# Loading q, k and v as float32 on the SP queue with casts on chip, and moving the x transposes a step earlier, in an attention-then-mixing kernel

## The chip, the cores and the metric

The kernel runs on one core of one Trainium2 chip. The metric is the device time of that core in microseconds (us), lower is better. Times are medians of several runs of the same kernel. The experiments ran in four sets on four chips, each set beside the kernel before on the same chip. A run more than 1.5% above the fastest of its kernel counts as slow and is left out. A profile covers one execution; its span, from the first to the last instruction, is about 1.7 us shorter than the time of the same execution (358.8 against 360.54 us in the changed kernel).

Names used below: PE is TensorE, PEld its weight load, DVE is VectorE, ACT is ScalarE, POOL is GpSimd, SP is SyncE (here it only issues transfers). Of the tiles, `ip` is a constant (an identity and the columns that average over 4 tokens), `pstr` is q or k transposed, `pd` the exponentials of the pooled attention and `xd` its output, `psS` the local attention scores, `pm` their exponentials, which GpSimd masks with two "selects" each, `psloc` the local attention output, `x` the sum of both attentions, `xT` its transpose, `psth` the theta product, `cs` its cosine and sine, `z` is x times `cs`, `psu` the mixing over tokens, `uT` the sum of mixing and xT, `psr` the last product.

## The reference

Eight batches, 8 heads, 576 tokens, head size 64. Two attentions are added, then a mixing layer follows:

```python
# attention 1: q, k, v averaged over groups of 4 tokens, full softmax attention, repeated 4 times
q_d = q.reshape(B, H, Sd, 4, D).mean(axis=3)          # the same for k, v
out_up = np.repeat(sm_attn(q_d, k_d, v_d), 4, axis=2)
# attention 2: local, a token sees the tokens at a distance under 4
mask = np.abs(pos[:, None] - pos[None, :]) < 4
out_local = softmax(where(mask, q @ k.T / 8, -1e9)) @ v
x = (out_up + out_local).transpose(0, 2, 1, 3).reshape(B, S, H * D)
# the mixing layer
theta = x @ w_theta
y = w_tok_r @ (x * cos(theta)) + w_tok_i @ (x * sin(theta))
u = x + y
return u + maximum(u @ w_ch, 0)
```

All inputs and the output are float32. The kernel computes in bfloat16 with float32 accumulation.

## The kernel before

Attention of batch b+1, `modulate` of batch b (theta and z) and `mix` of batch b-1 are three generators, interleaved in the fixed order of `PERIOD`: m, a and x stand for one step of `modulate`, `attention` and `mix`. The parts that the change and the argument touch:

```python
    def load(b):
        q_tm = work.tile([TR, NTR, H, D], BF16, tag="q_tm", name=f"q_tm{b}")
        k_tm = work.tile([TR, NTR, H, D], BF16, tag="k_tm", name=f"k_tm{b}")
        v_w = work.tile([P, NCH, H, 66], BF16, tag="v_w", name=f"v_w{b}")
        for dst, src in ((q_tm, q), (k_tm, k)):
            for c in range(NTR):
                nc.gpsimd.dma_start(
                    out=dst[:, c, :, :],
                    in_=src[b, :, TR * c:TR * c + TR, :].rearrange("h p d -> p h d"),
                )
        for c in range(NCH):
            nc.gpsimd.dma_start(
                out=v_w[0:KW[c], c, :, 0:D],
                in_=v[b, :, KS[c]:KS[c] + KW[c], :].rearrange("h p d -> p h d"),
            )
        nc.vector.memset(v_w[:, :, :, 64:65], 1.0)
        return q_tm, k_tm, v_w

    inputs = {0: load(0)}

    ident = const.tile([P, P], BF16, name="ident")
    nc.gpsimd.memset(ident, 0.0)
    nc.gpsimd.affine_select(out=ident, in_=ident, compare_op=ALU.not_equal, fill=1.0,
                            base=0, pattern=[[-1, P]], channel_multiplier=1)

    ip = const.tile([TR, TW], BF16, name="ip")
    nc.vector.tensor_copy(out=ip[:, 0:TR], in_=ident[0:TR, 0:TR])
    nc.gpsimd.memset(ip[:, TR:TW], 0.25)
    nc.gpsimd.affine_select(out=ip[:, TR:TW], in_=ip[:, TR:TW], compare_op=ALU.is_ge, fill=0.0,
                            base=0, pattern=[[-4, TP]], channel_multiplier=1)
    nc.gpsimd.affine_select(out=ip[:, TR:TW], in_=ip[:, TR:TW], compare_op=ALU.is_ge, fill=0.0,
                            base=3, pattern=[[4, TP]], channel_multiplier=-1)
    # ... pooling matrices PM and repeat matrices RT: 6 and 2 tiles, 24 + 4 selects on GpSimd ...
    wth = wpool.tile([P, 4, DM], BF16, name="wth")
    nc.gpsimd.dma_start(out=wth, in_=moe_w_theta.rearrange("(c p) e -> p c e", p=P))
    wtmp = ctx.enter_context(tc.tile_pool(name="wtmp", bufs=1))
    w_tm = []
    for ri, w_dram in enumerate((moe_w_tok_r, moe_w_tok_i)):
        t = wtmp.tile([P, 5, S], BF16, name=f"wtm{ri}")
        nc.gpsimd.dma_start(out=t[:, 0:4, :], in_=w_dram[0:512, :].rearrange("(c p) e -> p c e", p=P))
        nc.gpsimd.dma_start(out=t[0:64, 4, :], in_=w_dram[512:576, :])
        w_tm.append(t)
    wch = wpool.tile([P, 4, DM], BF16, name="wch")
    nc.gpsimd.dma_start(out=wch, in_=moe_w_ch.rearrange("(c p) e -> p c e", p=P))
```

The transfers that GpSimd issues here turn float32 into bfloat16 on their way: a piece of q lands as 96 KB, where the changed kernel's float32 piece has 192 KB. In `attention`, the local scores are masked like this, and only then multiplied with v:

```python
    def attention(b):
        q_tm, k_tm, v_w = inputs.pop(b)
        if b + 1 < B:
            inputs[b + 1] = load(b + 1)
        # ... transposes pstr, pooled attention ...
        for c in range(NCH):
            # ... psS matmuls, pm = exp(psS) on ACT ...
            nc.gpsimd.affine_select(out=pm[0:kw, :, 0:qn], in_=pm[0:kw, :, 0:qn],
                                    compare_op=ALU.is_ge, fill=0.0,
                                    base=off, pattern=[[0, 8], [-1, qn]], channel_multiplier=1)
            nc.gpsimd.affine_select(out=pm[0:kw, :, 0:qn], in_=pm[0:kw, :, 0:qn],
                                    compare_op=ALU.is_ge, fill=0.0,
                                    base=6 - off, pattern=[[0, 8], [1, qn]], channel_multiplier=-1)
            pms.append(pm)
            yield
        # ... psnd; then for each of 5 blocks psup, psloc, rl, tmp, x ...
```

The transposes of x, theta and z, and the order of a period:

```python
    def modulate(b):
        xT = moep.tile([P, 4, S], BF16, tag="xT", bufs=3, name=f"xT{b}")
        z = moep.tile([P, NCH, 2, DM], BF16, tag="z", name=f"z{b}")
        state[b] = (xT, z)
        xt = xs.pop(b)
        for c in range(NCH):
            cnt = QC[c]
            ps = w1(f"xTps{c}_{b}", BF16)[:, 0:512].rearrange("p (e t) -> p e t", e=4)
            for dc in range(4):
                nc.tensor.transpose(
                    out=ps[:, dc, 0:cnt],
                    in_=xt[c][0:cnt, P * dc:P * dc + P],
                    identity=ident[0:cnt, 0:cnt],
                )
            nc.vector.tensor_copy(out=xT[:, :, QS[c]:QS[c] + cnt], in_=ps[:, :, 0:cnt])
            yield
            th = w1(f"psth{c}_{b}")
            for dc in range(4):
                nc.tensor.matmul(
                    out=th[0:cnt, :],
                    lhsT=xT[:, dc, QS[c]:QS[c] + cnt],
                    rhs=wth[:, dc, :],
                    start=(dc == 0), stop=(dc == 3),
                )
            cs = moep.tile([P, 2, DM], BF16, tag="cs", bufs=3, name=f"cs{c}_{b}")
            nc.scalar.activation(out=cs[0:cnt, 0, :], in_=th[0:cnt], func=AF.Sin, bias=pihc[0:cnt], scale=1.0)
            nc.scalar.activation(out=cs[0:cnt, 1, :], in_=th[0:cnt], func=AF.Sin, bias=0.0, scale=1.0)
            nc.vector.tensor_tensor(
                out=z[0:cnt, c, :, :], in0=cs[0:cnt],
                in1=xt[c][0:cnt].unsqueeze(1).to_broadcast([cnt, 2, DM]),
                op=ALU.mult,
            )
            yield

    PERIOD = (
        "m a a m x m a a m x m a a m x m a a m x m a m "
        "a x a a a x a a x a a x a x a x a a x a a x a a x a x a"
    ).split()
    # ...
    a0 = attention(0)
    wt = build_WT()
    for _ in range(10):
        next(a0, 0)
        next(wt, 0)
    drain(wt)
    drain(a0)
    for b in range(B + 1):
        run(attention(b + 1) if b + 1 < B else None,
            modulate(b) if b < B else None,
            mix(b - 1) if b >= 1 else None)
```

The softmax here doesn't subtract the row's maximum and nothing guards it: scores larger than these inputs give would overflow.

## Time and profile before

The median is 365.32 us (four runs, 365.04 to 365.76). I cut the span at the first `psth` of each batch. That gives a start-up, seven periods, and a tail; in each period the attention of one batch, the theta of the one before and the mixing of the one before that are done together.

This is the view of busy time by stretch of the kernel before, for the start-up, the first period and one steady period. The columns are from:to, length, then the busy time of PE, PEld, DVE, ACT and POOL with the number of instructions, the mean granted PE clock (1.00 is full), the DMA engines' busy time as a share of the stretch (it can read over 1, as 1.19 and 1.35 below), and GB/s.

```profile
0.00:61.80 61.80, 27.81 (x247) 20.37 (x248) 15.64 (x43) 14.12 (x19) 53.23 (x98) 0.88 1.19 99
61.80:92.50 30.70, 23.16 (x239) 16.18 (x236) 16.69 (x41) 20.61 (x31) 30.59 (x37) 0.72 1.35 86
...
206.98:244.29 37.31, 33.77 (x346) 22.67 (x349) 21.70 (x53) 24.00 (x36) 23.56 (x28) 1.00 0.85 80
```

In the steady period PE is busy 33.77 of 37.31 us, and no other engine is near that. So PE sets the pace there, and what counts is where PE waits. In the start-up POOL is the busy one. GpSimd's own transfer issues are counted as busy here: of its 28 instructions in the steady period ten are selects, the rest issues.

The view of waits of the kernel before (who waited for whom, us in all, times, longest) shows the two waits that the change aims at: theta waits for the copy of the transposed x, and the very first transposes wait for a constant that GpSimd builds late.

```profile
PE pstr L177 <- POOL ip L102: 16.6, 1, 16.6
PE psth L352 <- DVE xT L348: 14.2, 15, 1.9
```

The timeline of its start (start, us, engine, line, operation, tile) shows why that constant is late: GpSimd issues 17 loads first.

```profile
1.37 4.74 POOL L77 DMA_DIRECT2D q_tm<-in_q_dram  x6 [0.84 <-POOLq L457]
...
10.63 4.48 POOL L82 DMA_DIRECT2D v_w<-in_v_dram  x5
...
16.64 1.36 PE L177 MATMUL pstr<-ip,q_tm 96*128 96x120 bf16 x12 [16.64 <-POOL ip L102]
...
24.77 0.79 POOL L136 DMA_DIRECT2D wth<-in_moe_w_theta_dram  x1
...
49.93 2.19 POOL L260 TENSOR_SCALAR_AFFINE_SELECT pm<-pm 128x1024 bf16<-128x1024 bf16 x2
```

Last, the chain of waits in the first period of the kernel before. ACT works almost without a break from 62.8 us on; the last of it, from the table load at 74.29, is below. Then come the selects, with a single load issue between them.

```profile
74.29 1.28 ACT L224
...
75.59 1.67 ACT pd L224 x2
...
77.79 1.03 ACT pm L254
...
78.89 2.13 POOL pm L260 x2
...
88.05 0.73 POOL k_tm L77
88.78 0.85 POOL pm L263
```

### The profile page before, as it was taken

What the parts mean: (1) busy time and instruction counts of PE and PEld (TensorE: products, weight loads), DVE (VectorE), ACT (ScalarE), POOL (GpSimd) and SP (SyncE); (2) the same over time, 40 slices, a digit from 0 to 9 for tenths busy, and PEclk for the clock granted to TensorE, in tenths of its full rate; (3) what the DMA queues carried; (4) which work ended last, traced back from release to release, by engine and by line L of the source; (5) the groups of instructions that cost most, each with busy time, mean ns of one, the idle gap of its engine ahead of it and who ended that gap; (6) DMA issues with size and microseconds to landing.
All of it is one profiled execution on the core that took longest, in us unless ns stands there. A gap on an engine that the chain in (4) does not pass through costs nothing.

```text
span 363.3 us, 6945 instructions
## 1 busy us (share of the span) xinstructions
PE 293.9 (81%) x2820; PEld 199.3 (55%) x2834; DVE 180.7 (50%) x428; ACT 191.3 (53%) x280; POOL 202.5 (56%) x267
## 2 busy tenths in 40 slices
PE   0162966948989978997999799979997899789995
PEld 0152643636665656565656465647564666456672
DVE  0020327617451875277536853594449444934433
ACT  1070331990569366845685567646774677323303
POOL 8996599999873957395639655870073006400000
PEclk9999955975699999999999999999999999989999
DMA  9909993991997199919991699057002000300303
GB/s 77 121 6 189 167 100 26 125 127 11 114 83 49 60 133 82 60 60 118 89 65 60 98 112 65 31 109 63 2 24 93 16 0 3 117 16 2 115 16 131
DMA packets 123392, 26.65 MB, mean 73 GB/s; under 512 B 116576, under 2 KB 118752, under 8 KB 123360
## 3 DMA queue, kind: packets, MB, share of 16 engines
q0 software_dynamic: 118112, 16.77, 66.7%
q1 hardware_dynamic: 5248, 9.44, 7.2%
q8 instruction: 22, 0.36, 0.4%
q14 instruction: 10, 0.08, 0.1%
HBM read 33.51 MB, written 9.44 MB: 118 GB/s over the span
## 4 chain that ended last, share of the span: by engine, by line
PE 45%; DVE 17%; ACT 15%; POOL 14%; issue 4%; DMA 4%; DVEq 0%; POOLq 0%
PE psu L377 16%; PE psth L352 10%; PE psr L395 5%; DVE tmp L319 4%; DVE osb L407 4%; DMA wch<-in_moe_w_ch_dram 4%; ACT pd L224 3%; DVE x L326 3%; ACT cs L359 3%; PE psS L247 3%; POOL pm L260 3%; POOL k_tm L77 3%; ACT L224 2%; PE pstr L177 2%; PE psvd L199 2%
## 5 line engine op out<-in xcount | busy, mean ns | idle before, releaser
L377 PE MATMUL psu<-WT,z 122*128 122x288 bf16 (+1 forms) x640 | 94.2, 292 | 0.0
L260 POOL TENSOR_SCALAR_AFFINE_SELECT pm<-pm 128x1024 bf16<-128x1024 bf16 (+1 forms) x40 | 40.7, 1038 | 71.4 <-ACT pm L254 71.3
L377 PEld LDWEIGHTS <-z 122*128 122x128 bf16 (+1 forms) x640 | 60.0, 99 | 23.8 <-issue 0.5
L352 PE MATMUL psth<-wth,xT 128*122 128x512 bf16 (+1 forms) x160 | 44.6, 402 | 14.2 <-DVE xT L348 14.2
L405 ACT ACTIVATE rel<-psr 128x512 f32<-128x512 f32 (+1 forms) x40 | 23.8, 596 | 57.4 <-PE psr L395 57.4
L386 DVE TENSOR_TENSOR uT<-psu,xT 128x288 bf16<-128x288 f32 x64 | 27.3, 454 | 53.2 <-PE psu L377 53.2
L184 ACT CAST qT<-pstr 128x576 bf16<-128x576 f32 x32 | 19.8, 640 | 55.6 <-PE pstr L177 55.6
L77 POOL DMA_DIRECT2D q_tm<-in_q_dram x48 | 37.0, 789 | 15.4 <-PE pstr L177 10.0
L361 DVE TENSOR_TENSOR z<-cs,x 122x1024 bf16<-122x1024 bf16 (+1 forms) x40 | 27.4, 686 | 34.3 <-ACT cs L360 34.3
L77 POOL DMA_DIRECT2D k_tm<-in_k_dram x48 | 36.8, 779 | 13.0 <-PE pstr L177 10.1
L395 PE MATMUL psr<-wch,uT 128*128 128x512 bf16 (+1 forms) x146 | 40.5, 380 | 2.3 <-DVE x L326 1.6
L254 ACT ACTIVATE pm<-psS 128x1024 bf16<-128x1024 f32 (+1 forms) x40 | 35.3, 976 | 12.5 <-PE psS L247 12.0
L263 POOL TENSOR_SCALAR_AFFINE_SELECT pm<-pm 128x1024 bf16<-128x1024 bf16 (+1 forms) x40 | 40.7, 1038 | 0.4
L82 POOL DMA_DIRECT2D v_w<-in_v_dram x40 | 35.4, 913 | 9.7 <-PE psloc L310 7.3
L359 ACT ACTIVATE cs<-psth,pihc 122x512 bf16<-122x512 f32 (+1 forms) x40 | 27.6, 691 | 23.7 <-PE psth L352 23.3
L352 PEld LDWEIGHTS <-xT 128*122 128x122 bf16 (+1 forms) x160 | 18.4, 135 | 26.4 <-DVE xT L348 18.3
L177 PE MATMUL pstr<-ip,q_tm 96*128 96x120 bf16 x192 | 16.4, 236 | 19.7 <-POOL ip L102 16.6
L407 DVE TENSOR_TENSOR osb<-rel,psx 128x512 f32<-128x512 f32 (+1 forms) x40 | 27.3, 682 | 7.9 <-ACT rel L405 7.1
L319 DVE TENSOR_TENSOR tmp<-psloc,rl 122x512 bf16<-122x512 f32 (+1 forms) x40 | 26.5, 687 | 0.3
L310 PEld LDWEIGHTS <-pm 128*128 128x128 bf16 (+1 forms) x320 | 17.0, 112 | 17.3 <-POOL pm L263 8.0
L348 DVE COPY xT<-xTps 128x488 bf16<-128x488 bf16 (+1 forms) x40 | 15.6, 391 | 21.1 <-PE xTps L343 21.1
L326 DVE TENSOR_TENSOR x<-tmp,psup 122x512 bf16<-122x512 bf16 (+1 forms) x40 | 25.9, 673 | 0.0
(62 smaller groups left out, 407.8 us busy)
## 6 DMA issues: line engine op xcount, KB each, us to landing
out_dram<-osb SPq DMA_DIRECT2D x32, 256.0 KB, 2.0
q_tm<-in_q_dram POOLq DMA_DIRECT2D x48, 96.0 KB, 3.7
k_tm<-in_k_dram POOLq DMA_DIRECT2D x48, 96.0 KB, 3.7
v_w<-in_v_dram POOLq DMA_DIRECT2D x32, 128.0 KB, 4.7
out_dram<-osb SPq DMA_DIRECT2D x8, 128.0 KB, 3.2
v_w<-in_v_dram POOLq DMA_DIRECT2D x8, 91.0 KB, 5.3
wtm<-in_moe_w_tok_r_dram POOLq DMA_DIRECT2D x1, 576.0 KB, 8.4
wtm<-in_moe_w_tok_i_dram POOLq DMA_DIRECT2D x1, 576.0 KB, 10.3
```

The lines of the kernel that those rows point to most:

```text
L77: nc.gpsimd.dma_start(out=dst[:, c, :, :], in_=src[b, :, TR * c:TR * c + TR, :].rearrange("h p d -> p h d"),)
L82: nc.gpsimd.dma_start(out=v_w[0:KW[c], c, :, 0:D], in_=v[b, :, KS[c]:KS[c] + KW[c], :].rearrange("h p d -> p h d"),)
L254: nc.scalar.activation(out=pm[0:kw, :, 0:qn], in_=ps[0:kw].rearrange("p e (j w) -> p (e j) w", w=P)[:, :, 0:qn], func=AF.Exp, scale=SCL,)
L260: nc.gpsimd.affine_select(out=pm[0:kw, :, 0:qn], in_=pm[0:kw, :, 0:qn], compare_op=ALU.is_ge, fill=0.0, base=off, pattern=[[0, 8], [-1, qn ...
L263: nc.gpsimd.affine_select(out=pm[0:kw, :, 0:qn], in_=pm[0:kw, :, 0:qn], compare_op=ALU.is_ge, fill=0.0, base=6 - off, pattern=[[0, 8], [1, ...
L319: nc.vector.tensor_tensor(out=tmp[0:cnt].rearrange("p (j e d) -> p e j d", e=2, j=4), in0=pv[0:cnt, :, :, 0:D], in1=rl[0:cnt].unsqueeze(3) ...
L326: nc.vector.tensor_tensor(out=x[0:cnt], in0=tmp[0:cnt], in1=up[0:cnt], op=ALU.add)
L352: nc.tensor.matmul(out=th[0:cnt, :], lhsT=xT[:, dc, QS[c]:QS[c] + cnt], rhs=wth[:, dc, :], start=(dc == 0), stop=(dc == 3),)
L359: nc.scalar.activation(out=cs[0:cnt, 0, :], in_=th[0:cnt], func=AF.Sin, bias=pihc[0:cnt], scale=1.0)
L377: nc.tensor.matmul(out=pss[hf][:, 0:288], lhsT=z[0:QC[c], c, ri, P * dc:P * dc + P], rhs=WT[0:QC[c], ri, c, 288 * hf:288 * hf + 288], star ...
L395: nc.tensor.matmul(out=psr[0:cnt, :], lhsT=uT[:, dc, OS[c]:OS[c] + cnt], rhs=wch[:, dc, :], start=(dc == 0), stop=(dc == 3),)
L407: nc.vector.tensor_tensor(out=osb[0:cnt], in0=rel[0:cnt], in1=psx[0:cnt, 0:DM], op=ALU.add)
```

## The change

It has four parts. The loads of q, k and v go to the SP queue as float32 into staging tiles. They are cast on chip: for batch 0 by VectorE, GpSimd and ScalarE, for the other batches by GpSimd. That frees GpSimd of 17 load issues a batch. The constants are built as three tiles, two pooling matrices (`PU`) and one repeat matrix (`ru`), which replace the eight old ones with the help of shifted views. The views need blocks of 120 tokens, which replace those of 122. And the transposes of x run one step ahead of theta, with a new `PERIOD`, so that theta need not wait for the copy of its own transposes.

```diff
-QS = [0, 122, 244, 366, 488]
+QS = [0, 120, 240, 360, 480]
 (QC, KS, KW, QN likewise)
 ...
-    def load(b):
-        (17 nc.gpsimd.dma_start a batch, into bfloat16 tiles)
+    def load_qk(b):
+        ts = []
+        for nm, src in (("q", q), ("k", k)):
+            t = work.tile([TR, NTR, H, D], FP32, tag=f"{nm}32", bufs=1, name=f"{nm}32_{b}")
+            for i in range(2):
+                for c in range(3 * i, 3 * i + 3):
+                    nc.sync.dma_start(
+                        out=t[:, c, :, :],
+                        in_=src[b, :, TR * c:TR * c + TR, :].rearrange("h p d -> p h d"),
+                    )
+            ts.append(t)
+        staged[b] = ts
 (load_v: the same for v, five pieces)
+    def cast(b, engines):
+        q32, k32, v32 = staged.pop(b)
+        q_tm = work.tile([TR, NTR, H, D], BF16, tag="q_tm", bufs=1, name=f"q_tm{b}")
 ...
+        for eng, dst, src in ((engines[0], q_tm, q32), (engines[1], k_tm, k32)):
+            for i in range(2):
+                eng(out=dst[:, 3 * i:3 * i + 3], in_=src[:, 3 * i:3 * i + 3])
+                yield
 (three casts of v, after 2 yields)
 ...
+    first = cast(0, (nc.vector.tensor_copy, nc.gpsimd.tensor_copy, nc.scalar.copy))
+    for _ in range(4):
+        next(first)
     wth = wpool.tile([P, 4, DM], BF16, name="wth")
     nc.gpsimd.dma_start(out=wth, in_=moe_w_theta.rearrange("(c p) e -> p c e", p=P))
 (then the constants: PU with 7 selects and ru with 2, in place of PM and RT; then the token and channel weights)
 ...
     def attention(b):
         q_tm, k_tm, v_w = inputs.pop(b)
         if b + 1 < B:
-            inputs[b + 1] = load(b + 1)
+            load_qk(b + 1)
+            load_v(b + 1)
+        ahead = cast(b + 1, (nc.gpsimd.tensor_copy,) * 3) if b + 1 < B else iter(())
 (next(ahead, 0) in the steps of psnd and of psloc)
 ...
     def modulate(b):
-        for c in range(NCH):
+        def transposes(c):
             (xTps, xT)
-            yield
+        transposes(0)
+        yield
+        for c in range(NCH):
+            cnt = QC[c]
+            if c + 1 < NCH:
+                transposes(c + 1)
             (psth, cs, z)
 ...
     PERIOD = (
-        "m a a m x m a a m x m a a m x m a a m x m a m "
-        "a x a a a x a a x a a x a x a x a a x a a x a a x a x a"
+        "m a m a a x m a x m a a x m a x m a "
+        "a a x a a x a a x a a x a a x a x a a x a x a a x"
     ).split()
 ...
-    for _ in range(10):
-        next(a0, 0)
-        next(wt, 0)
-    drain(wt)
-    drain(a0)
+    drain(first)
+    drain(attention(0))
+    wt = build_WT()
+    drain(wt)
```

Before, GpSimd issued the weights after its 17 loads and all its constants. Now it has no loads to issue.

## The prediction

> **What bounds the kernel now.** In the chain of waits the first theta products (psth) of successive batches start at 61.9, 92.5, 132.4, 169.7, 207.0, 244.3, 281.7 and 318.7 us; the end is at 363.3. So: start-up 61.9, first period 30.6, second 39.9, five steady periods of 37.3, tail 44.6.
> - Start-up is bound by GpSimd. In the timeline its first 17 load issues run to 15.1 us, before the identity is made; PE transposes nothing until 16.6 us (waits: pstr on POOL's ip). Then the token weights are waited for (8.0 us), and batch 1's load issues precede batch 0's mask selects, which run only from 49.9 to 60.7 us.
> - First period: POOL is busy 30.6 of 30.7 us (busy time by stretch): 10.3 us of selects, the rest load issues.
> - Steady period: PE busy 33.8 of 37.3 us; POOL 23.6, ACT 24.0, DVE 21.7. Of PE's idle time theta waiting for the copy of the transposed x is 1.9 us a period, 14.2 in all.
>
> **What the change does.**
> - Removes 109 us of load issues from POOL (13.6 a batch: 12 of about 0.79, 5 of about 0.9), and some 5 us of constant building.
> - Adds casts: 3072 + 3072 + 2560 elements a partition and batch. No trace has a GpSimd cast; at the select's rate (1092 ns for 1024) I estimate 9.3 us a batch, range 8 to 13. POOL falls from 23.6 to about 20 us a period. [...]
> - Loads keep about 14,000 packets a batch, now 256 B written, not 128. At the start about as many landed in some 18 us at about 90% busy engines; estimate 18 to 28 us a batch, inside a period.
> - Moves xT transposes a step earlier: takes the 1.9 us away.
> - 120-token blocks: work about unchanged.
>
> **On the critical path.**
> - Start-up: q lands by about 8 us, transposes at about 9, selects from about 20 to 32, token-weight transposes (10 x about 0.9 us) after. First psth at about 44 us (38 to 52): minus 18.
> - First period: no load issues before the selects: 27. Second: 37.5.
> - Five steady periods at 35.5 (34.5 to 36.5): minus 9.
> - Tail: minus 2.
> Sum: 44 + 27 + 37.5 + 177.5 + 42.5 = 328.5 us of span, 330.5 as time. I add some for re-ordered work and a colder clock early (granted 0.72 in the first period): 333.
>
> **What would show it.** POOL with no DMA issues after the weights; a cast at 1.5 to 2.2 us for 1536 elements; pstr near 9 us; first psth at 38 to 52 us; psth <- DVE xT under 4 us in all; steady period 34.5 to 36.5 with PE over 93% busy; POOL about 20 us a period.
>
> **What would make it wrong.**
> - Casts far slower than selects, or held up by VectorE: [...] Then pstr waits on casts at each period's start, as q_tm and k_tm are single-buffered.
> - 256-byte packets slower on SP's queue, so a batch takes over 35 us: DMA sets the period, and outputs queue behind loads on SP.
> - Casts placed before the selects, delaying psloc.
> - q, k and v landing late at the start.
>
> Chances: faster by over 2% 0.91, within 2% 0.06, slower 0.03. Time 333 us, 318 to 350.

## The result, and the profile after

The changed kernel takes 360.27 us (four runs, 359.47 to 361.1) against 365.32 us. The ratio is 0.986, with a 95% interval of 0.984 to 0.989: within 2%. Ratios are computed as the mean time of one kernel's fast runs over that of the other's of the same rounds, so they are not quite the ratio of the medians quoted. The prediction was 333 us, with a range of 318 to 350, so the time lies outside it.

The busy time by stretch of the changed kernel: start-up, first period, and two steady periods.

```profile
0.00:63.37 63.37, 30.90 (x258) 22.13 (x258) 19.37 (x53) 18.64 (x25) 29.55 (x41) 1.00 1.07 176
63.37:96.75 33.38, 24.20 (x229) 16.89 (x229) 16.81 (x39) 18.53 (x28) 17.72 (x16) 0.71 0.62 102
...
172.74:210.57 37.83, 34.90 (x348) 23.43 (x348) 24.85 (x53) 23.80 (x36) 19.41 (x17) 0.95 0.83 154
210.57:246.63 36.06, 33.53 (x348) 22.58 (x349) 23.26 (x53) 23.74 (x36) 21.38 (x18) 1.00 0.85 164
```

POOL did fall, as it should: 53.2 to 29.6 us in the start-up and 23.6 to about 20 us in a period. But the start-up is not shorter, the first period is longer, and the steady periods are of two lengths. Against the prediction (spans, us):

| stretch | before | changed | predicted | changed minus predicted |
|---|---|---|---|---|
| start-up | 61.9 | 63.4 | 44 | +19.4 |
| first period | 30.6 | 33.4 | 27 | +6.4 |
| second period | 39.9 | 38.3 | 37.5 | +0.8 |
| five steady periods | 186.3 | 183.1 | 177.5 | +5.6 |
| tail | 44.6 | 40.7 | 42.5 | -1.8 |
| span | 363.3 | 358.8 | 328.5 | +30.3 |

The five steady periods are 37.74, 37.83, 36.06, 36.07 and 35.41 us.

**The start-up.** The timeline of the changed kernel:

```profile
0.81 8.69 SPq L80 DMA_DIRECT2D q<-in_q_dram  x6
...
1.31 0.88 POOL L139 DMA_DIRECT2D wth<-in_moe_w_theta_dram  x1 [0.80 <-POOLq L498]
...
8.83 0.80 POOL L178 DMA_DIRECT2D wch<-in_moe_w_ch_dram  x1
9.53 14.93 SPq L80 DMA_DIRECT2D k<-in_k_dram  x6
10.66 0.96 DVE L106 CAST q_tm<-q 96x1536 bf16<-96x1536 f32 x1 [8.00 <-DMA q<-in_q_dram]
...
19.46 0.96 DVE L106 CAST q_tm<-q 96x1536 bf16<-96x1536 f32 x1 [7.74 <-DMA q<-in_q_dram]
...
25.32 1.46 POOL L106 CAST k_tm<-k 96x1536 bf16<-96x1536 f32 x1 [15.70 <-DMA k<-in_k_dram]
...
41.53 2.13 POOL L295 TENSOR_SCALAR_AFFINE_SELECT pm<-pm 128x1024 bf16<-128x1024 bf16 x2 [11.52 <-ACT pm L289]
```

GpSimd issues the first weight at 1.31 us and the last at 8.83, while q and k are still on their way; before, the first weight was issued at 24.77. The weights are 4.75 MB in float32 (twice 512 x 512 and twice 576 x 576, 4 bytes each), four times q of one batch. The second half of q lands only at 19.5 us, where I had all of q by about 8. SP itself is held: its twelve issues for q and k take 23.6 us. So far this is a coincidence in time; experiment e3 tests it.

**The waits** of the changed kernel: theta's wait for xT is halved, to one of about 1.0 us a period, at the period's start. A small wait is new: the mixing matmuls wait for `uT`, which VectorE makes.

```profile
PE psth L396 <- DVE xT L386: 6.8, 6, 1.7
PE psu L421 <- DVE uT L430: 2.5, 5, 0.5
```

**VectorE and GpSimd.** The view of tile z gives the durations (least, median, greatest, ns), first in the kernel before, then in the changed one.

```profile
L361 DVE TENSOR_TENSOR z<-cs,x x40: 680/683/694, 66.3 to 334.3; 122x1024 bf16<-122x1024 bf16 x32, 88x1024 bf16<-88x1024 bf16 x8
```

```profile
L405 DVE TENSOR_TENSOR z<-cs,x x40: 675/692/2565, 68.6 to 329.8; 120x1024 bf16<-120x1024 bf16 x32, 96x1024 bf16<-96x1024 bf16 x8
```

The timeline of both engines in one period of the changed kernel shows two of the long ones and a short one before them. Here are the DVE lines, then the POOL lines:

```profile
177.83 0.68 DVE L405 TENSOR_TENSOR z<-cs,x 120x1024 bf16<-120x1024 bf16 x1
...
180.03 1.77 DVE L405 TENSOR_TENSOR z<-cs,x 120x1024 bf16<-120x1024 bf16 x1
...
188.17 2.56 DVE L405 TENSOR_TENSOR z<-cs,x 96x1024 bf16<-96x1024 bf16 x1 [0.52 <-ACT cs L404]
```

```profile
177.85 3.40 POOL L106 CAST q_tm<-q 96x1536 bf16<-96x1536 f32 x2 [9.67 <-PE pstr L212]
...
187.32 2.88 POOL L106 CAST k_tm<-k 96x1536 bf16<-96x1536 f32 x2 [4.29 <-PE pstr L212]
```

The first long z ends at 181.80, and the pair of casts beside it at 181.25; the second ends at 190.73, its pair of casts at 190.20. Both times z ends some 0.54 us after the casts, as if it could start in earnest only then. In this kernel it went by who started first: the five z that began 0.02 us before a cast took 0.68 us each, the 14 that began while a cast ran took 0.92 to 2.56 us. The short z above is one of the five. It began at 177.83 us, 0.02 us before the first cast of q; that cast took 1.99 us instead of the usual 1.46.

**The clock.** In two of the steady periods the granted clock is 0.95. By stretch, it is one piece of 3.4 us at half clock, right after the period's start:

```profile
172.98:176.40 3.42, 3.42 (x17) 2.19 (x16) 0.54 (x3) 2.42 (x4) 0.00 (x0) 0.50 1.05 207
176.40:177.50 1.10, 1.10 (x15) 0.95 (x14) 0.00 (x0) 0.00 (x0) 0.00 (x0) 1.00 1.39 196
```

A busy PE loses half of 3.4 us in it, 1.7 us (in e1 below, the steady period with such a piece took 37.07 us, the others 35.40 or 35.41). The other such piece is at 135.5 to 138.8 us. The kernel before has one outside its start-up and first two periods, at the start of its tail (319.9 us).

**The first period.** The chain of waits of the changed kernel, from the same table load on:

```profile
77.61 1.28 ACT L259
...
78.90 1.67 ACT pd L259 x2
...
81.27 1.03 ACT pm L289
...
82.36 2.13 POOL pm L295 x2
```

The selects begin 19.0 us after the period's start, where they began 17.0 us after it in the kernel before. They wait for ACT in both.

### The profile page after: what moved, and what is told of

Its sections match the earlier page's. It is cut to its first block, busy times and chain, and to the rows that moved or that the text cites. A ratio compares the mean times of both kernels' runs of the same rounds, so it can differ in the third digit from the quotient of the medians.

```text
span 358.8 us, 7037 instructions
## 1 busy us (share of the span) xinstructions
PE 296.6 (83%) x2834; PEld 201.8 (56%) x2834; DVE 193.5 (54%) x435; ACT 192.1 (54%) x283; POOL 156.2 (44%) x153
## 3 DMA queue, kind: packets, MB, share of 16 engines
q0 software_dynamic: 2272, 2.38, 4.0%
## 4 chain that ended last, share of the span: by engine, by line
PE 47%; DVE 20%; ACT 15%; SPq 7%; issue 4%; POOL 3%; DMA 3%; POOLq 0%; ACTq 0%
PE psu L421 18%; PE psth L396 9%; SPq L80 6%; PE psr L439 6%; DVE osb L451 4%; DVE tmp L355 4%; DVE z L405 4%; DVE x L362 4%; PE pstr L212 3%; ACT pd L259 3%; PE psS L282 3%; ACT L259 2%; PE psnd L311 2%; PE wps L187 2%; ACT vd L240 2%
## 5 line engine op out<-in xcount | busy, mean ns | idle before, releaser
L421 PE MATMUL psu<-WT,z 120*128 120x288 bf16 (+1 forms) x640 | 93.6, 292 | 2.5 <-DVE uT L430 2.5
L421 PEld LDWEIGHTS <-z 120*128 120x128 bf16 (+1 forms) x640 | 60.5, 100 | 23.2 <-issue 3.6
L295 POOL TENSOR_SCALAR_AFFINE_SELECT pm<-pm 128x1024 bf16<-128x1024 bf16 (+1 forms) x40 | 41.2, 1047 | 65.5 <-ACT pm L289 65.5
L449 ACT ACTIVATE rel<-psr 128x512 f32<-128x512 f32 (+1 forms) x40 | 23.8, 596 | 61.7 <-PE psr L439 61.7
L396 PE MATMUL psth<-wth,xT 128*120 128x512 bf16 (+1 forms) x160 | 45.1, 406 | 7.6 <-DVE xT L386 6.8
L405 DVE TENSOR_TENSOR z<-cs,x 120x1024 bf16<-120x1024 bf16 (+1 forms) x40 | 39.1, 977 | 17.4 <-ACT cs L404 17.3
L403 ACT ACTIVATE cs<-psth,pihc 120x512 bf16<-120x512 f32 (+1 forms) x40 | 27.5, 687 | 35.8 <-PE psth L396 35.6
L106 POOL CAST k_tm<-k 96x1536 bf16<-96x1536 f32 x16 | 24.5, 1547 | 41.6 <-DMA k<-in_k_dram 17.5
L106 POOL CAST q_tm<-q 96x1536 bf16<-96x1536 f32 x14 | 23.2, 1679 | 40.5 <-PE pstr L212 32.2
L396 PEld LDWEIGHTS <-xT 128*120 128x120 bf16 (+1 forms) x160 | 20.5, 139 | 17.3 <-DVE xT L386 8.1
L386 DVE COPY xT<-xTps 128x480 bf16<-128x480 bf16 (+1 forms) x40 | 15.5, 389 | 25.7 <-PE xTps L381 25.6
L355 DVE TENSOR_TENSOR tmp<-psloc,rl 120x512 bf16<-120x512 f32 (+1 forms) x40 | 26.9, 685 | 0.1
L362 DVE TENSOR_TENSOR x<-tmp,psup 120x512 bf16<-120x512 bf16 (+1 forms) x40 | 26.5, 675 | 0.0
```

What stands on the lines that cost most here:

```text
L106: eng(out=dst[:, 3 * i:3 * i + 3], in_=src[:, 3 * i:3 * i + 3])
L355: nc.vector.tensor_tensor(out=tmp[0:cnt].rearrange("p (j e d) -> p e j d", e=2, j=4), in0=pv[0:cnt, :, :, 0:D], in1=rl[0:cnt].unsqueeze(3) ...
L362: nc.vector.tensor_tensor(out=x[0:cnt], in0=tmp[0:cnt], in1=up[0:cnt], op=ALU.add)
L396: nc.tensor.matmul(out=th[0:cnt, :], lhsT=xT[:, dc, QS[c]:QS[c] + cnt], rhs=wth[:, dc, :], start=(dc == 0), stop=(dc == 3),)
L405: nc.vector.tensor_tensor(out=z[0:cnt, c, :, :], in0=cs[0:cnt], in1=xt[c][0:cnt].unsqueeze(1).to_broadcast([cnt, 2, DM]), op=ALU.mult,)
L421: nc.tensor.matmul(out=pss[hf][:, 0:288], lhsT=z[0:QC[c], c, ri, P * dc:P * dc + P], rhs=WT[0:QC[c], ri, c, 288 * hf:288 * hf + 288], star ...
```

## The experiments

Thirteen runs were made, e9 with the changed kernel itself. Theories and rivals, as they stood after reading the traces, with the letters that the recorded expectations use:

- The whole: the new order of steps is the useful part, and the load path takes much of it back (A). Rival: the order alone gives little, or something other than the load path holds the periods up.
- Start-up: the weights, issued early, take the transfers' bandwidth from q and k (B). Rival: 256-byte pieces on the SP queue are simply slow.
- Steady periods: casts on GpSimd hold up z on VectorE (C). Rival: the half-clock pieces alone make the periods longer, for a reason of their own.
- The half-clock pieces come from PE being too idle around the period's start (D). Rivals: they belong to the load path, or they fall at random.

Here are all thirteen beside the two kernels. All figures are us; the columns after the time are the stretches of the profiled run, with the mean of the five steady periods. The kernel before took 365.32 us beside the changed kernel, and 364.44, 364.89, 365.12 and 365.31 in the sets of e1 to e4, e5 to e8, e9 to e12 and e13. So differences of times across sets carry an error of up to about 0.9 us, which the ratios take out.

| kernel | time | ratio | start-up | first | second | steady | tail |
|---|---|---|---|---|---|---|---|
| before | 365.32 | 1 | 61.9 | 30.6 | 39.9 | 37.3 | 44.6 |
| changed | 360.27 | 0.986 | 63.4 | 33.4 | 38.3 | 36.6 | 40.7 |
| e1 | 353.46 | 0.968 | 61.7 | 31.8 | 37.4 | 35.7 | 42.3 |
| e2 | 353.62 | 0.970 | 62.3 | 30.0 | 36.7 | 36.1 | 42.4 |
| e3 | 345.14 | 0.947 | 49.7 | 31.4 | 38.6 | 36.2 | 42.3 |
| e4 (wrong result) | 354.19 | 0.972 | 62.9 | 31.3 | 37.4 | 35.7 | 42.2 |
| e5 | 346.41 | 0.950 | 63.1 | 35.4 | 35.5 | 34.8 | 38.8 |
| e6 | 354.47 | 0.973 | 65.5 | 30.4 | 36.9 | 36.1 | 42.8 |
| e7 | 346.13 | 0.950 | 55.7 | 33.1 | 37.5 | 35.4 | 40.7 |
| e8 | 338.82 | 0.930 | 60.3 | 32.6 | 33.5 | 33.8 | 39.3 |
| e9 (changed, one look) | 360.56 | | 63.2 | 33.5 | 38.3 | 36.6 | 40.7 |
| e10 | 334.38 | 0.915 | 51.0 | 34.6 | 35.0 | 34.8 | 38.8 |
| e11 | 332.17 | 0.912 | 50.1 | 33.6 | 35.5 | 34.6 | 38.7 |
| e12 | 338.25 | 0.927 | 61.8 | 34.0 | 33.5 | 33.8 | 38.8 |
| e13 | 327.52 | 0.896 | 49.2 | 35.0 | 33.5 | 33.8 | 39.1 |

In e5, e8 and e10 to e13 a step of the mixing stands before the first `psth` of a batch, from batch 1 on. That moves the cut between stretches: their first period is longer and their tail shorter by this alone, so these two columns can't be held against those of the other kernels.

### e1: the new order alone

The kernel before, with only the transposes a step ahead and the new `PERIOD`; loads, constants and blocks are the old ones.

```diff
 (against the kernel before)
-        for c in range(NCH):
+        def transposes(c):
             ...
+        transposes(0)
+        yield
+        for c in range(NCH):
+            if c + 1 < NCH:
+                transposes(c + 1)
 (and the PERIOD of the changed kernel)
```

> The kernel before with only the x transposes one step ahead and the new order of steps; loads, constants and blocks as before. Theory A (the reordering is the useful part, the load path eats it): start-up stays at about 62 us to the first psth, steady period about 35.5 us instead of 37.3, tail about 41 instead of 44.6; time 351 us (347 to 356), so faster than the whole change (360.3). Rival (the whole is needed, the reorder alone gives about 1 us a period and the tail little): 358 to 362 us.

It took 353.46 us, ratio 0.968 (0.962 to 0.974), beside 364.44 us for the kernel before in the same rounds. This part alone gives more than the whole change. Four of the five steady periods are 35.40 or 35.41 us, and the fifth, 37.07, holds a half-clock piece. So the 35.5 us that I predicted for the steady period is right for the order of steps, and half-clock pieces come without the new load path too (against that rival of D).

### e2: the changed kernel with the old loads

```diff
 (against the changed kernel)
-    load_qk(0)
-    load_v(0)
+    inputs[0] = load(0)          # the old load(): 17 casting transfers from GpSimd
 ...
-            load_qk(b + 1)
-            load_v(b + 1)
-        ahead = cast(b + 1, (nc.gpsimd.tensor_copy,) * 3) if b + 1 < B else iter(())
+            inputs[b + 1] = load(b + 1)
+        ahead = iter(())
```

> The changed kernel with the loads of before (GpSimd queue, cast in flight, two buffers), no casts by engines; everything else of the change kept. Theory A: z goes back to about 0.69 us each, no long z; steady period about 35.5; start-up about 60 us; time 350 us (345 to 356). Rival (the load path is a gain and something else in the change, the blocks or the order of steps, holds the period at 36 to 38): 360 us or more, period at 36 to 38 us.

It took 353.62 us, ratio 0.970 (0.966 to 0.975). It differs from e1 by the blocks, the constants and the place of the weight transposes in the start, and in time by 0.2 us: those parts are worth nothing that these runs could show. And it differs from the changed kernel by the load path alone, so in this kernel the new load path costs 6.7 us (5.7 by the ratios). That is theory A.

### e3: the weights after k

One element of each weight tile is written from the last piece of k of batch 0 before its load is issued. The load overwrites it, so the result is the same, but the load waits for that piece of k: the first weight is issued at 16.63 us, below, after k's second cast has begun at 15.2 us.

```diff
 (against the changed kernel)
+    hold = staged_k0[0:1, NTR - 1, 0, 0:1]
     wth = wpool.tile([P, 4, DM], BF16, name="wth")
+    nc.vector.tensor_copy(out=wth[0:1, 0, 0:1], in_=hold)
     nc.gpsimd.dma_start(out=wth, ...)
 (the same for the token weights, two writes each, and for wch)
```

> The changed kernel, with the loads of the weights made to wait for the last k piece of batch 0 (a one-element copy into each weight tile). Theory B (at the start the weights' 4.6 MB share the 16 DMA engines with q and k): q landed by about 8 to 10 us instead of 19.5, k by 14 to 17 instead of 28.5, first psth at 50 to 54 us instead of 63.4, time 349 us (345 to 353). Rival (the SP queue issues or moves 256-byte rows slowly by itself): q at 15 us or later, first psth over 58 us, time within 3 us of 360.

It took 345.14 us, ratio 0.947 (0.942 to 0.952): 15.1 us less than the changed kernel. The start-up is 49.7 us, 13.7 less. The timeline of its start, to be held against that of the changed kernel:

```profile
0.81 3.92 SPq L80 DMA_DIRECT2D q<-in_q_dram  x6
...
4.77 6.12 SPq L80 DMA_DIRECT2D k<-in_k_dram  x6
...
6.00 0.95 DVE L106 CAST q_tm<-q 96x1536 bf16<-96x1536 f32 x1 [3.34 <-DMA q<-in_q_dram]
...
12.05 1.46 POOL L106 CAST k_tm<-k 96x1536 bf16<-96x1536 f32 x1 [6.77 <-DMA k<-in_k_dram]
...
16.63 0.89 POOL L142 DMA_DIRECT2D wth<-in_moe_w_theta_dram  x1
...
27.63 2.13 POOL L301 TENSOR_SCALAR_AFFINE_SELECT pm<-pm 128x1024 bf16<-128x1024 bf16 x2 [6.74 <-ACT pm L295]
```

The queue, the pieces and the casts are the same; only the weights start later. Yet the first cast of q moves from 10.66 to 6.00 us, that of k from 25.32 to 12.05, and SP's twelve issues take 10.1 us in place of 23.6. That settles B against its rival for 13.7 of the 19.4 us.

### e4: casts that write but don't read

For batches 1 to 7 each cast becomes a cast of one column, which keeps every wait, and a fill that writes the whole tile. The result is wrong on purpose (relative error 0.98).

```diff
 (against the changed kernel)
+        def write_only(out, in_):
+            nc.gpsimd.tensor_copy(out=<first column of out>, in_=<first column of in_>)
+            nc.gpsimd.memset(out, 0.01)
-        ahead = cast(b + 1, (nc.gpsimd.tensor_copy,) * 3) ...
+        ahead = cast(b + 1, (write_only,) * 3) ...
```

> The changed kernel, each later GpSimd cast replaced by a cast of one column and a memset of the whole destination: same order on PE, DVE, ACT and SP, result wrong on purpose. Theory C (the cast's reads hold up z[...]): z's mean falls from 977 to about 690 ns, no z over 0.8 us; steady periods with casts fall from 36.1 to 37.8 to about 35.3 us; time 354 us (350 to 357). Rival (z was slow for another reason, or its length is off the path): z stays over 0.9 us on average, or z falls and the time stays within 2 us of 360.

It took 354.19 us, ratio 0.972 (0.969 to 0.976). PE, VectorE, ACT and SP run the same instructions in the same order as in the changed kernel. The view of tile z in this run:

```profile
L409 DVE TENSOR_TENSOR z<-cs,x x40: 680/690/693, 68.6 to 323.6; 120x1024 bf16<-120x1024 bf16 x32, 96x1024 bf16<-96x1024 bf16 x8
```

No z is longer than 693 ns, and the steady periods are 35.40 to 35.42 us, but for one of 37.06 with a half-clock piece. So it is the reading of GpSimd's casts that holds up z (up to 2565 ns with the casts, up to 693 ns with fills in their place, though the view does not show which z ran beside a fill), and it costs 0.66 us a period (36.06 against 35.40): theory C. Its rival is half right: the pieces at half clock account for the rest of the excess. What costs is not the longest z. In the changed kernel the period with z of 1.77 and 2.56 us is only 0.1 us longer than the one before it with 1.77 and 1.21, and the first steady period of e3, where only the last z of five is long (1.21 us), is 35.41 us. So the cost comes with the second z of a period.

The half-clock pieces did not go away but moved (238.4 and 310.1 us, in place of 135.5 and 173.0), although PE's instructions are the same. I come back to that at e9.

### e5: the first mixing step before the first theta

```diff
 (against the changed kernel)
-        "m a m a a x m a x m a a x m a x m a "
+        "m x a m a a m a x m a a x m a x m a "
```

> The changed kernel with one edit in the order of steps: the first step of the token mix (psu, which waits for nothing of this period) is moved ahead of the first theta. Theory D (the half-clock stretches of 3.4 us after a period's start come from the PE doing only transposes and waiting there for about 3 us): no granted clock below 0.9 in the steady periods, where the changed kernel lost 1.7 us in two of them; and the wait of theta for the xT copy (1.0 us a period) is filled. Steady period 35.0 us (34.4 to 35.6), time 353 us (350 to 356). Rival (the clock dips at random, or the end of each period is set by VectorE alone): dips remain in one or two periods, period 36 us or more, time 357 to 361.

It took 346.41 us, ratio 0.950 (0.946 to 0.954), 13.9 us less than the changed kernel and below the range that I expected. It puts a mixing step of twelve matmuls (the trace has 14 `psu` there), which need nothing new, where PE waits for the period's first xT. Four of the five steady periods are well below the floor of 35.4 us (34.44, 34.71, 34.72 and, in the last, 33.71; the fourth is 36.57), and no half-clock piece lies at any period's start: for D. The 36.57 was a surprise. It has no half-clock piece, but a z of 3.08 us (e10 has the like: 3.08 us, in a period of 36.63). The DVE line and the POOL line:

```profile
240.13 3.08 DVE L405 TENSOR_TENSOR z<-cs,x 120x1024 bf16<-120x1024 bf16 x1 [0.27 <-ACT cs L404]
```

```profile
239.80 2.87 POOL L106 CAST q_tm<-q 96x1536 bf16<-96x1536 f32 x2 [7.93 <-PE pstr L212]
```

z began 0.33 us after a pair of back-to-back casts had, and ended at 243.21, again 0.54 us after their end. So it was held through both.

### e6: GpSimd loads again from batch 1 on

e3, with the SP path for batch 0 only. The float32 staging was moved into the buffers of z, which are free at the start.

```diff
 (against e3)
-            load_qk(b + 1)
-            load_v(b + 1)
-        ahead = cast(...)
+            inputs[b + 1] = load_sw(b + 1)       # the old load()
+        ahead = iter(())
```

> The late weights (e3), SP loads and engine casts for batch 0 only, and the loads of before (GpSimd queue, cast in flight) for batches 1 to 7. Theory A+B+C: start-up as in e3 (first psth near 49.7 us), z at 0.69 us, steady period 35.4, time 341 us (337 to 344), so 3 to 4 us under e3. Rival (batch 1's GpSimd issues now stand before batch 0's selects as in the kernel before): first psth at 55 us or later, time 346 or more.

It took 354.47 us, ratio 0.973 (0.967 to 0.978): a miss. The start-up, 65.5 us in the profiled run (357.6 us, the longest of the four), lost everything that e3 had won. The reason is the same one again: GpSimd, with nothing to hold it back, issued the loads of batch 1 from 4.86 us on, and they competed with k and v of batch 0. The timeline shows SP held at v's issues, v's last piece cast at 40.85 us, and the selects after it:

```profile
12.10 12.86 SPq L108 DMA_DIRECT2D v<-in_v_dram  x5
...
40.85 0.62 ACT L129 CAST v_w<-v 100x512 bf16<-100x512 f32 x1 [6.87 <-DMA v<-in_v_dram]
44.26 2.13 POOL L318 TENSOR_SCALAR_AFFINE_SELECT pm<-pm 128x1024 bf16<-128x1024 bf16 x2 [5.49 <-ACT pm L312]
```

GpSimd was idle before that select, so it was not its own issues that made it late, which I had held possible. That it is the competition is tested by e13, which takes batch 1 off GpSimd's queue, and with it both its issues there and its overlap with batch 0.

### e7: casts on VectorE

```diff
 (against e3)
-        ahead = cast(b + 1, (nc.gpsimd.tensor_copy,) * 3) ...
+        ahead = cast(b + 1, (nc.vector.tensor_copy,) * 3) ...
```

> e3 with the casts of batches 1 to 7 on VectorE instead of GpSimd (it took 0.95 us for the 1536-element piece at the start, GpSimd 1.46). Theory C says z returns to 0.69 us since no GpSimd instruction reads SBUF beside it but the selects; VectorE gets about 5.7 us more a period (21.5 to 27 of 36). Time 343 us (340 to 347), within 3 us of e3, better only if VectorE's work at the period's end is not delayed; selects may grow from 1.09 us where a cast runs beside them. Rival (VectorE is what ends the period): period over 37 us, time over 350.

It took 346.13 us in its three fast runs (345.77 to 347.31; a fourth, 352.12, was slow and is left out), ratio 0.950 (0.947 to 0.953), not to be told from e3 (0.942 to 0.952). The steady periods are all 35.40 us, and z is 677 to 694 ns. So C holds from the other side too: with no GpSimd cast beside it, z keeps its time. What it won there it lost in the start-up, 55.7 us against 49.7, where the casts of batch 1 stand in VectorE's line among the work of batch 0. The first of them starts at 36.74 us, after VectorE waited 15.5 us for q of batch 1; batch 0's `xd` stands behind it, and PE waits 6.1 us, once, for that.

### e8: e6 with the mixing step first and the weight transposes interleaved

```diff
 (against e6: the PERIOD of e5, and)
-    drain(attention(0))
+    a0 = attention(0)
     wt = build_WT()
+    for _ in range(14):
+        next(a0, 0)
+    for _ in range(10):
+        next(a0, 0)
+        next(wt, 0)
     drain(wt)
+    drain(a0)
```

> e6 with the mix step first (e5) and the token-weight transposes interleaved into batch 0's attention where PE idles, as the kernel before had them. If the causes add up: first psth at 43 to 46 us (the 8 us of token-weight transposes after attention hidden for the most part), steady period 34.4 to 35.4 with no clock dip, tail 42: time 332 us (328 to 338). Rival (they overlap): 338 to 343.

It took 338.82 us, ratio 0.930 (0.927 to 0.933). The steady periods are 33.7 to 33.8 us: with no casts on chip after batch 0 and the mixing step first, the wait, the z delay and the half-clock pieces are all gone. The start-up, 60.3 us where 43 to 46 were expected, still has e6's fault, so the time missed its range (328 to 338).

### e9: the changed kernel once more

No edit; one look.

> The changed kernel unaltered, another look. If the half-clock stretches come from a window that runs free of the program (theory D), they fall in other periods this time or in another number of them; each costs 1.7 us. If they fall in the same two periods (those that start at 135 and 173 us) again, something in those periods' instructions causes them. Time 359 to 361.5 us.

It took 360.56 us, with the same periods within 0.1 us, and half-clock pieces in the same two periods. By the expectation this speaks for a cause in those periods' instructions and against a window that runs free of the program. To see more I listed where the pieces begin in every run with more than one after the second period's start, divided by 3.4133 us. This spacing is an estimate from the runs themselves: by the mean clock of slices of 0.1 us, the outer pieces of e2 begin at 129.246 and 310.152 us and those of e6 at 133.234 and 314.140, both 180.906 us apart, which is 53 times 3.4133 us; a piece itself lasts 3.41 us (172.99 to 176.41 us in the changed kernel). The remainders, with the beginnings read in steps of 0.1 us:

| run | pieces begin near (us) | remainder (us) |
|---|---|---|
| changed | 135.5, 173.0 | 2.38, 2.33 |
| e9 | 135.5, 173.0 | 2.38, 2.33 |
| e1 | 237.5, 309.2 | 1.98, 2.00 |
| e2 | 129.3, 272.6, 310.2 | 3.01, 2.95, 3.00 |
| e3 | 263.8, 301.3 | 0.98, 0.93 |
| e4 | 238.4, 310.1 | 2.88, 2.90 |
| e6 | 133.3, 276.6, 314.2 | 0.18, 0.12, 0.18 |

Within each run the remainders agree to 0.1 us over up to 53 steps (the outer two of e2 and of e6 by construction). So the pieces lie on a fixed grid of 3.413 us, and the phase of the grid differs from run to run (remainders from 0.1 to 3.0 us). It explains how e4, with the same PE instructions, has its pieces in other periods: its periods have other lengths, and so meet the grid elsewhere. So e9 decided less than I had expected of it. Why the changed kernel and e9 met it in the same phase is open.

And it shows what the grid meets. PE's busy time in the 3.4 us before a period's first theta, first in the changed kernel, then in e12 (the columns are from:to, length, PE busy and count, clock, DMA, GB/s):

```profile
169.34:172.74 3.40, 2.12 (x27) 1.00 0.70 187
```

```profile
227.40:230.80 3.40, 3.32 (x40) 1.00 1.19 140
```

2.12 of 3.40 us, mostly small transposes: my estimate is that a half-clock piece follows where a step of the grid falls right on this, and not where the step also takes in the dense work on either side. The traces bear this out in part. The changed kernel, e1 to e4, e6, e7 and e9, all without the mixing step first, have 40 steady periods. In 11 of them a step of the grid began 2.9 to 3.2 us before the first theta, and these 11 have a half-clock piece at their start; the other 29 have none. So e7 had no piece although it has the old order: its steps began at other times. But the busy time of a step alone does not decide: steps that began 2.4 to 2.8 us before the first theta hold 2.13 to 2.18 us as well, and in the kernel before two that began 2.93 and 3.17 us before it hold 1.98, with no piece after any of them. With the mixing step first PE is busy for 3.32 of 3.40, and none of e5, e8, e10, e11, e12, e13 has a piece at a period's start. What lowers the clock was not shown.

### e10: weights after k, and the mixing step first

e3 and e5 together.

> e3 and e5 together: weights late and the mix step first, casts still on GpSimd. If the two causes are separate, the gains add (15 + 14 us): first psth near 50 us, steady periods 34.4 to 34.7, with z still over 0.85 us on average; time 332 us (329 to 336). If they overlap: 338 or more.

It took 334.38 us, ratio 0.915 (0.911 to 0.919). e3 gained 15.1 us, e5 13.9, 29.0 in sum; together they gain 25.9, most of it, as they act on different stretches. It shows how much of the loss was in these two: the prediction was 333 us.

### e11: casts of batches 2 to 7 on VectorE

```diff
 (against e10, with the interleaving of e8)
-        ahead = cast(b + 1, (nc.gpsimd.tensor_copy,) * 3) ...
+        ahead = cast(b + 1, (nc.gpsimd.tensor_copy if b == 0 else nc.vector.tensor_copy,) * 3) ...
```

> e10 with the casts of batches 2 to 7 on VectorE (batch 1's stay on GpSimd) and the token-weight transposes interleaved into batch 0's attention. z at 0.69 us in the steady periods, these at 33.7 to 34.2 us, no clock dip; first psth at 43 to 47 us. Time 322 us (318 to 328). If VectorE's added 5.7 us a period lands at the period's end, where it is busy throughout: steady period 35 or more and 330 us or more.

It took 332.17 us, ratio 0.912 (0.908 to 0.915). Three of its steady periods are 34.71 us, as e10 has 34.61 and 34.72 with GpSimd's casts; e12 has 33.81 with no casts. So once PE is dense, the casts cost about 0.9 us in such a period on either engine, against casting transfers. The time was a miss: I had expected 322 us (318 to 328), with periods of 33.7 to 34.2 and a start-up of 43 to 47. The start-up is 50.1 us, and e10 has 51.0, so interleaving the weight transposes gained little here.

### e12: the order alone, with the mixing step first

e1 with the `PERIOD` of e5: none of the load path, constants or blocks of the change.

> e1 (the kernel before with only the reordering) with the mix step first as well. No load path, no constants, no blocks of the change. Steady period 33.8 us as in e8, no clock dip in six periods, start-up 61.9; time 340 us (336 to 343). Rival (mix first gains only where casts hold up z): 350 us or more.

It took 338.25 us, ratio 0.927 (0.925 to 0.929). A change of 27 us without touching a load.

### e13: each part where it pays

Batches 0 and 1 by SP with casts, batches 2 to 7 by casting loads from GpSimd; weights after k; the mixing step first. This answers e6: batch 1's issues now stand behind batch 0's in SP's line.

```diff
 (against e6, with the PERIOD of e5)
-            inputs[b + 1] = load_sw(b + 1)
-        ahead = iter(())
+            if b == 0:
+                load_qk(1)
+                load_v(1)
+            else:
+                inputs[b + 1] = load_sw(b + 1)
+        ahead = cast(1, (nc.gpsimd.tensor_copy,) * 3) if b == 0 else iter(())
```

> Weights late and mix step first; batches 0 and 1 loaded on SP and cast by engines, batches 2 to 7 loaded by GpSimd with the cast in flight as in the kernel before. If the two parts of the explanation are right and separate, it has the start-up of e3 (first psth at 49 to 52 us, where e6 and e8 had 65.5 and 60.3 because batch 1's issues stood before batch 0's selects) and the steady period of e12 (33.8 us, no z over 0.75 us, no half-clock stretch after 100 us): 50 + 33 + 34 + 5 x 33.8 + 38.8 = 325 us of span, time 327 us (323 to 331). If GpSimd issues of batch 2 hold up batch 1's selects, the first period is 36 us or more and the time 332 or more.

It took 327.52 us, ratio 0.896 (0.894 to 0.899), with a correct result: the best of all, 37.8 us below the 365.31 of the kernel before in its rounds and 32.8 below the changed kernel. The start-up is 49.2 us, as in e3, though batches 2 to 7 are loaded by GpSimd as in e6: what e6 lost was the overlap of batch 1 with batch 0. The steady period is 33.8 us. The expectation was met, but for the first period (35.0 us, 33 expected), which has one z of 1.04 us beside a cast. As e13 takes GpSimd's issues away too, the reading of e6's loss rests also on GpSimd's idle time there.

## Why the prediction was wrong

The prediction summed 328.5 us of span and got 358.8. It had "q, k and v landing late at the start" among its risks, but gave no cause and no time for it. By its own terms:

1. **"q lands by about 8 us ... First psth at about 44 us" failed; this is the step that cost most, 19.4 us.** I took the transfers' bandwidth for free at the start because the old profile had no other traffic there. It had none because the loads and constants on GpSimd kept the weights back until 24.8 us. Taking GpSimd's loads away also took away that order. e3 shows 13.7 of the 19.4 us to be the weights. The other 5.7 us stay in e3: k's two casts begin at 12.0 and 15.2 us, and ACT has kT and the casts of v (2.7 us) to do before it can start on the masks' input, so its selects run from 27.6 to 39.1 us and not from 20 to 32. I did not test these 5.7 us by themselves.

2. **"First period: no load issues before the selects: 27" failed, by 6.4 us.** I read "POOL is busy 30.6 of 30.7 us" as "POOL bounds this period". The chain of waits of the kernel before, shown above, says otherwise. ACT works until 78.82 us, and the selects that follow take 10.7 us with one load issue of 0.73 us among them. So at most 0.7 us was to be had. e2, with load issues, has 30.0 us here, and e4, with neither issues nor reading casts, 31.3; that of e2 is the shortest of all runs. In the changed kernel the selects began 2 us later in the period, where the chain goes through two z of 1.47 and 1.39 us, each beside a cast, and later two casts stand among the selects.

3. **"Five steady periods at 35.5" was right as the floor, and was missed by 5.6 us in all.** e1 and e4 have 35.40 us where nothing disturbs. Two periods lost 1.7 us each to a half-clock piece, and four lost 0.66 us each to z: together 6.0 us above the floor, which itself is 0.1 us a period under 35.5. The prediction named casts "held up by VectorE" as a risk, and feared that pstr would wait on them. One cast beside z did take 1.99 us instead of 1.46, but z was held up more, up to 2.56 us instead of 0.69, and what waited was PE's mixing, for `uT`, which stands behind z in VectorE's line (2.5 us in all in the view of waits). It did not foresee the clock in the steady periods at all, because the kernel before has 1.00 there.

4. **"psth <- DVE xT under 4 us in all" failed in size: 6.8.** One wait of 1.0 us a period remains. The transposes of the first block still come directly before its theta, as they have no earlier step to go to. e5 and e12 show that this leftover was the cheap thing to mend: e12 is 15.2 us faster than e1, by 1.6 to 1.7 us in an undisturbed steady period (PE is idle for 0.78 us of it, where it was 2.15), by the two pieces at half clock (1.7 us each) in e1's steady periods and tail, and by the rest in the second period and tail.

5. **The costs of the removed and added work were right.** A cast of 1536 elements took 1.46 us alone (1.55 to 1.68 in the mean), where I had 1.5 to 2.2. POOL came to about 20 us a period, as predicted, and PE to 93% of an undisturbed steady period (33.53 of 36.06 us). But POOL bounds no steady period, so there was nothing in it to win: e1 and e2 show that the order alone gives 11 to 12 us, and that the load path takes 6.7 of it back.

6. **The tail was better than predicted** by 1.8 us. The tail of the kernel before contained a half-clock piece (1.7 us), which I had taken as part of it; in the changed kernel's tail the clock falls only after PE's last work (that ends at 354.5 us; the clock is 1.00 to 357 us, then 0.66 and 0.50).

So the mechanism of the reorder was right and its size too. What failed is the start-up, where the freed engine sent its other work earlier, into the way of the first inputs.

What stays open: the phase of the clock's grid, the 5.7 us of the start-up, and the first period's floor of about 30 us, which I read from the chain but did not move by experiment.

## What to carry to other kernels

When you free an engine of work, ask what it does next and what that will collide with: here its weight loads moved 23 us forward, onto the first inputs, and holding them back by one tiny write each was worth 15 us. Before counting an engine's busy time as the limit of a stretch, follow the chain of waits through that stretch. And keep PE dense across the seam between periods: moving twelve ready matmuls into a 1 us wait gave 1.6 us in each undisturbed period, and took the half-clock pieces with it.
